# Pack attention and two MoE layers on one core: gate weights in a pool of their own, w_in conversions one per step

## The chip, the cores and the metric

The kernel runs on one core of a Trainium2 chip. The metric is the device time of one execution in microseconds (us); the median of three runs stands for a kernel. An execution was profiled besides; all rows shown come from it. The engines are TensorE (PE; its weight loads are PEld), VectorE (DVE), ScalarE (ACT), GpSimd (POOL) and SyncE (SP), which issues the DMAs.

## The reference

```python
p_packed = sm_attn(p, k, v)              # first attention: 32 packed queries a head, 576 keys
out = sm_attn(q, p_packed, p_packed)     # second attention: 576 queries, 32 packed keys
x = out.transpose(0, 2, 1, 3).reshape(4608, 512)
h = np.maximum(x @ w_in, 0.0)            # MoE 1: 512 -> 2048, squared relu
x = (h * h) @ w_out                      # 2048 -> 512
logits = x @ w_gate + modality_bias[modality_id]     # 8 experts
e_idx = np.argmax(logits, axis=1)
for e in range(8):                       # MoE 2, each token to one expert
    h = np.maximum(x[mask] @ w1[e], 0.0)
    out[mask] = gate_w[mask, None] * (h @ w2[e])
```

Batch 8, 8 heads of 64, 576 positions; 4608 tokens of 512. `w_in` and `w_out` come as float64, `w1` and `w2` as float32.

## The kernel before

**First attention.** The loop at L892 has 16 + 3 steps. `att1(i)` handles a "quad" (four heads of a batch) in four parts, one a step: scores `s` (L296), softmax (L307 to L314), transposes `ta` and `tb` (L319, L320), the product with the values `pq` (L328, L329) with its split into `pphl`. Step i does the scores of quad i and the `pq` of quad i - 3. SyncE loads keys three quads ahead (576 KB each) and values four ahead (576 KB). Keys lie in parts of `wgb` (the buffer of the gate weights, which are needed only later) and in `rows`; values lie in `early`, the memory that later becomes `ring`.

**Conversions.** The float64 weights are read as pairs of 32-bit integers, a 512 KB load for each [128, 512] tile, and `convert` (L197 to L215) rebuilds a float32 value (Square on ScalarE; L202, L205, L208 and L211 on VectorE) and splits it into `hi` (ScalarE, L214) and `lo` (GpSimd, L215). `conv_in` does 16 tiles of `w_in` into `wbt`, two in each of the first eight steps; at step 8 what is left of it is emitted and the tile `head` is allocated. `head` takes the memory of `stage`, which the conversions use as scratch. `conv_out` does the same for `w_out`, over the same slots of `wbt`, with buffers in `wgb` and `rows`; it follows behind the attention.

**Pack products.** `pw_unit(bp, u)` multiplies the packed attention of a pair of batches `bp` with tile `u` of `w_in`: three products (L360), a copy into `pws` (three buffers; on VectorE for odd pairs, L364, else on ScalarE, L366) and a write to DRAM. For pair 0 the halves go straight into the blocks `head` and `ring` (L375 on ScalarE, L376 on GpSimd), which layer 1 reads. The table `PW` says which units are placed in which step; `others(u)` makes what is missing ahead of and in the first token unit, with one `conv_out` step each. In the first attention all of `ta`, `tb`, `pq`, the scores of the second attention and `pw` share four PSUM banks.

**MoE 1** runs over 12 units of 384 tokens and 16 slices `f`: `layer1` (L472), relu and square, `layer2` (L492). `tail(u)` multiplies the rows of a unit with the eight gate weight rows in `wgb`; 24 products with a sum each (L515 on VectorE), then softmax and a write to DRAM; `route` and `tables` assign tokens to expert groups. For the last unit (u = 11), three of eight products a row block go to GpSimd (L519) with the sum on ScalarE (L520).

**MoE 2** runs over nine groups of 512 slots, each with one expert: `gathered` (tokens by indirect DMA, transposed into `xt`), `weights1` and `weights2` (load and split, L720 and L721), and `group`: eight `f` of 12 products (L784), whose relu is split into `ht` by ScalarE (L794) and VectorE (L795), then four times 24 products (L806), scaled into `o` (L815) and scattered (L817). Groups 0 to 6 take tokens of the first 28 of 36 tiles only, so that their tables are made before the last unit's routing.

**Order and memory.** The instructions of each engine are put in order when the kernel is built, by priority and a simulated time line; the order of the code is the priority, and `tc.high_priority` raises it (by 200 instructions for the whole of group 0, by 40 for `ht`). Each engine runs its own list strictly in that order. SBUF pools opened with side "left" stand on one another: ahead of the change `const`, `x2`, `raw`, then, until `st3.close()`, `pp` (`wgb` of 16 KB a partition and `pp32` of 8 KB), `at` and `g`; after that, in their place, `o` (16 KB) and `h` (32 KB). A pool that takes the place of closed ones waits until all instructions that use those are through.

Of the kernel before, what the change touches and what calls it, by code (L numbers as in the profile page):

```python
# [10 lines left out]
F32 = mybir.dt.float32  # L11
# [15 lines left out]
def tile_pack_attention_moe_moe2(  # L27
# [58 lines left out]
    w_p = ctx.enter_context(tc.tile_pool(name="raw", bufs=2, side="left"))  # L86
    pp_p = st3.enter_context(tc.tile_pool(name="pp", bufs=1, side="left"))
# [5 lines left out]
    wgb = pp_p.tile([P, NE, DM], F32, name="wgb")  # L93
# [126 lines left out]
    PW = {9 + i: [(0, 2 * i), (0, 2 * i + 1)] for i in range(4)}  # L220
    PW |= {13 + i: [(1, 2 * i), (1, 2 * i + 1)] for i in range(6)}
    for i in range(3):
        PW[16 + i].append((2, i))
    A20 = 4
# [126 lines left out]
    def pw_unit(bp, u, so=None):  # L351
# [11 lines left out]
        if bp % 2:  # L363
            nc.vector.tensor_copy(so, ph)  # L364
        else:
            nc.scalar.activation(out=so, in_=ph, func=AF.Copy)  # L366
# [140 lines left out]
    def tail(u):  # L507
        js = slice(u * UT, (u + 1) * UT)
        lg = lg_all[:, js, :]
        prod = held["g"].tile([P, DM], F32, tag="ghl", name="prod") if u == NUN - 1 else None  # L510
        for t in range(UT):
            for e in range(NE):
                one = lg[:, t, e : e + 1]
                if prod is None or e < 5:
                    nc.vector.scalar_tensor_tensor(  # L515
                        out=junk, in0=row[:, t, :DM], scalar=1.0, in1=wgb[:, e], op0=ALU.mult, op1=ALU.mult, accum_out=one
                    )
                else:
                    nc.gpsimd.tensor_tensor(out=prod, in0=row[:, t, :DM], in1=wgb[:, e], op=ALU.mult)  # L519
                    nc.scalar.activation(out=prod, in_=prod, func=AF.Copy, accum_out=one)  # L520
                if e % 2 == 1:
                    yield
# [249 lines left out]
    def group(g, more):  # L772
# [27 lines left out]
        for t in range(NTT):  # L800
# [13 lines left out]
            o = held["o"].tile([P, DM], F32, tag="o", name="o")  # L814
# [16 lines left out]
    def pull(gens, n=1):  # L831
        for _ in range(n):
            while gens:
                try:
                    next(gens[0])
                    break
                except StopIteration:
                    gens.pop(0)
# [53 lines left out]
    for i in range(len(quads) + 3):  # L892
# [10 lines left out]
        pull(cv, 2)  # L903
        if i == 8:
            pull(cv, NU)
            held["head"] = const.tile([P, HEAD, 2, NPC, P], F32R, tag="head", name="head")
# [88 lines left out]
    held["o"] = ctx.enter_context(tc.tile_pool(name="o", bufs=8, side="left"))  # L995
# [70 lines left out]
```

## Time and profile before

| what | us |
|---|---|
| median of three runs | 1307.05 (1306.3 to 1307.85) |
| the profiled execution | 1303.67 |
| its span, first to last instruction | 1301.9 |

| engine | busy us | share of the span |
|---|---|---|
| TensorE products | 1232.0 | 95% |
| TensorE weight loads | 1028.0 | 79% |
| VectorE | 811.6 | 62% |
| ScalarE | 607.1 | 47% |
| GpSimd | 336.8 | 26% |

Times in rows are us from the start of the span. "Busy" is the time in which an engine works on an instruction; the granted clock (PEclk) is the share of TensorE's full 2.4 GHz, so that 0.50 is 1.2 GHz. A timeline row merges like instructions that follow one another; `x12` are twelve of them; `<-` in brackets names what ended the wait ahead of it. In a stretch's row each engine's busy time is followed by its count of instructions.

### The profile page before, as it was taken

What the parts mean: (1) busy time and instruction counts of PE and PEld (TensorE: products, weight loads), DVE (VectorE), ACT (ScalarE), POOL (GpSimd) and SP (SyncE); (2) the same over time, 40 slices, a digit from 0 to 9 for tenths busy, and PEclk for the clock granted to TensorE, in tenths of its full rate; (3) what the DMA queues carried; (4) which work ended last, traced back from release to release, by engine and by line L of the source; (5) the groups of instructions that cost most, each with busy time, mean ns of one, the idle gap of its engine ahead of it and who ended that gap; (6) DMA issues with size and microseconds to landing.
All of it is one profiled execution on the core that took longest, in us unless ns stands there. A gap on an engine that the chain in (4) does not pass through costs nothing.

```text
span 1301.9 us, 18383 instructions
## 1 busy us (share of the span) xinstructions
PE 1232.0 (95%) x6356; PEld 1028.0 (79%) x6356; DVE 811.6 (62%) x2022; ACT 607.1 (47%) x1227; POOL 336.8 (26%) x398
## 2 busy tenths in 40 slices
PE   7899899999999999999999999929999999999995
PEld 4567777888888888888888888818788888888884
DVE  5886865849758694874867597875543444354341
ACT  3675565565555555455654556531433332343230
POOL 4663565322103231022310132040220221122011
PEclk8799999999999999999999999969999999999998
DMA  9876656332011221112121023320532542453210
GB/s 348 296 268 212 186 170 181 119 90 75 25 42 49 68 79 43 42 50 66 49 74 43 25 77 97 122 81 10 195 129 77 185 159 91 141 186 98 107 65 35
DMA packets 74167, 145.06 MB, mean 111 GB/s; under 512 B 6608, under 2 KB 26192, under 8 KB 73936
## 3 DMA queue, kind: packets, MB, share of 16 engines
q1 hardware_dynamic: 68304, 124.62, 29.9%
q0 software_dynamic: 5760, 19.17, 4.5%
q8 instruction: 52, 0.85, 0.3%
q14 instruction: 51, 0.42, 0.1%
HBM read 109.92 MB, written 33.85 MB: 110 GB/s over the span
## 4 chain that ended last, share of the span: by engine, by line
PE 84%; DVE 5%; DMA 4%; ACT 2%; POOL 2%; issue 2%; SPq 0%; POOLq 0%; ACTq 0%; DVEq 0%
PE acc L492 28%; PE ph L472 16%; PE h L784 15%; PE o L806 15%; PE pq L328 2%; PE s L427 2%; PE pw L360 2%; DMA wraw<-in_moe_w 2%; PE tr L764 1%; PE s L296 1%; POOL prod L519 1%; DMA wgb<-in_moe_w_out 1%; PE pq L329 1%; DMA rows<-in_moe_w_out 1%; PE ta L454 1%
## 5 line engine op out<-in xcount | busy, mean ns | idle before, releaser
L492 PE MATMUL acc<-wbt,ghl 128*128 128x512 f32 x1728 | 443.5, 399 | 0.0
L492 PEld LDWEIGHTS acc<-wbt,ghl 128*128 128x128 f32 x1728 | 315.9, 189 | 60.6 <-ACT ghl L483 0.4
L515 DVE SCALAR_TENSOR_TENSOR rows<-rows,wgb 128x512 f32<-128x512 f32 x279 | 218.9, 785 | 3.7
L784 PE MATMUL h<-xt,wbt 128*128 128x512 f32 x864 | 215.1, 399 | 0.7 <-DVE xt L768 0.4
L784 PEld LDWEIGHTS h<-xt,wbt 128*128 128x128 f32 x864 | 163.0, 189 | 40.3 <-DVE xt L768 0.7
L485 DVE TENSOR_TENSOR ghl<-r,ghl 128x384 fp32r<-128x384 f32 x176 | 108.0, 615 | 114.0 <-ACT ghl L483 113.2
L472 PE MATMUL ph<-a2T,ring 128*128 128x384 f32 (+1 forms) x840 | 145.7, 310 | 2.3 <-ACT ring L403 2.3
L483 ACT ACTIVATE ghl<-r 128x384 fp32r<-128x384 f32 x192 | 100.2, 522 | 97.5 <-PE acc L492 95.7
L472 PEld LDWEIGHTS ph<-a2T,ring 128*128 128x128 f32 x840 | 130.4, 191 | 10.6 <-ACT ring L403 2.8
L806 PE MATMUL o<-head,ht 128*128 128x512 f32 x432 | 113.9, 398 | 26.0 <-ACT ht L794 25.8
L481 ACT ACTIVATE r<-ph 128x384 f32<-128x384 f32 x192 | 92.9, 485 | 91.1 <-PE ph L472 85.1
L795 DVE SCALAR_TENSOR_TENSOR ht<-h,ht 128x512 fp32r<-128x512 f32 x72 | 49.3, 688 | 124.2 <-ACT ht L794 124.1
L472 PE MATMUL ph<-a2T,head 128*128 128x384 f32 (+1 forms) x696 | 119.4, 308 | 0.0
L806 PEld LDWEIGHTS o<-head,ht 128*128 128x128 f32 x432 | 81.2, 190 | 45.2 <-issue 26.2
L817 POOL DMA_INDIRECT out<-o,idx_s x36 | 36.7, 1018 | 299.3 <-DVE o L815 293.7
L806 PE MATMUL o<-ring,ht 128*128 128x512 f32 x432 | 112.2, 395 | 0.0
L794 ACT ACTIVATE ht<-h 128x512 fp32r<-128x512 f32 x72 | 42.5, 593 | 148.8 <-PE h L784 148.8
L472 PEld LDWEIGHTS ph<-a2T,head 128*128 128x128 f32 x696 | 106.5, 190 | 6.3
L482 ACT ACTIVATE r<-r 128x384 f32<-128x384 f32 x192 | 99.9, 522 | 4.1
L404 POOL TENSOR_TENSOR ring<-praw,ring 128x256 fp32r<-128x256 f32 x62 | 52.2, 843 | 168.8 <-ACT ring L403 123.6
L806 PEld LDWEIGHTS o<-ring,ht 128*128 128x128 f32 x432 | 80.3, 188 | 16.8
L721 DVE TENSOR_TENSOR wbt<-wraw,wbt 128x1024 fp32r<-128x1024 f32 x36 | 44.1, 1225 | 50.0 <-ACT wbt L720 49.8
(213 smaller groups left out, 1482.7 us busy)
## 6 DMA issues: line engine op xcount, KB each, us to landing
wraw<-in_moe_w SPq DMA_DIRECT2D x72, 512.0 KB, 3.7
praw<-pw_d SPq DMA_DIRECT2D x56, 256.0 KB, 3.9
pw_d<-pws SPq DMA_DIRECT2D x48, 256.0 KB, 3.1
x_d<-rows SPq DMA_DIRECT2D x12, 792.0 KB, 4.0
qT<-in_q SPq DMA_DIRECT2D x36, 256.0 KB, 3.7
early<-in_v SPq DMA_DIRECT2D x16, 512.0 KB, 6.6
rows<-in_k SPq DMA_DIRECT2D x10, 576.0 KB, 6.3
wgb<-in_moe_w_out SPq DMA_DIRECT2D x11, 512.0 KB, 4.5
```

What stands on the lines that cost most here:

```text
L404: nc.gpsimd.tensor_tensor(out=t[:, 1], in0=raw, in1=t[:, 0].bitcast(F32), op=ALU.subtract)
L472: nc.tensor.matmul(ph[:, off : off + n], t[:, x, c, :], a[:, y, c, off : off + n], start=(i == 0), stop=(i == 3 * NPC - 1),)
L481: nc.scalar.activation(out=r, in_=ph, func=AF.Relu)
L482: nc.scalar.activation(out=r, in_=r, func=AF.Square)
L483: nc.scalar.activation(out=hl[:, 0], in_=r, func=AF.Copy)
L485: eng.tensor_tensor(out=hl[:, 1], in0=r, in1=hl[:, 0].bitcast(F32), op=ALU.subtract)
L492: nc.tensor.matmul(acc[t], hl[:, x, t * P : (t + 1) * P], wbt[:, f, y, :], start=(f == 0 and x == 0 and y == 0), stop=(f == NF - 1 and x = ...
L515: nc.vector.scalar_tensor_tensor(out=junk, in0=row[:, t, :DM], scalar=1.0, in1=wgb[:, e], op0=ALU.mult, op1=ALU.mult, accum_out=one)
L721: nc.vector.tensor_tensor(out=t[:, 1, :], in0=raw, in1=t[:, 0, :].bitcast(F32), op=ALU.subtract)
L784: nc.tensor.matmul(ph, half1[:, g % 2, c, x, f * P : (f + 1) * P], xs[c][:, y, :], start=(i == 0), stop=(i == 3 * NDC - 1),)
L795: nc.vector.scalar_tensor_tensor(out=h[:, 1, :], in0=ph, scalar=0.0, in1=h[:, 0, :].bitcast(F32), op0=ALU.max, op1=ALU.subtract)
L806: nc.tensor.matmul(po, hs[f][:, x, t * P : (t + 1) * P], second(f)[:, y, :], start=(i == 0), stop=(i == 3 * NFE - 1),)
```

## The change

The gate weights `wgb` get a pool of their own, `wg`, ahead of `pp`, which stays open to the end; `o` in MoE 2 uses the eight 2 KB slices of `wgb` in turn and its own pool goes. The last unit's 24 gate products are all on VectorE. One `w_in` conversion is emitted a step instead of two, to the end of step 15; what follows in `head` comes at step 16. In `PW`, pair 1's units 0 to 11 stand in steps 11 to 16; pair 0's units 0 to 3 and pair 2's units 0 and 1 in steps 17 and 18 (before: pair 0's units 0 to 7 in steps 9 to 12, pair 1's units 0 to 11 in 13 to 18, pair 2's 0 to 2 in 16 to 18). The copies into `pws` are all on ScalarE during the first attention. The second attention of unit 0 starts at step 6 instead of 4.

```diff
--- before.py
+++ after.py
@@ -84,13 +84,14 @@
     st2 = ExitStack()
     st3 = ExitStack()
     w_p = ctx.enter_context(tc.tile_pool(name="raw", bufs=2, side="left"))
+    wg_p = ctx.enter_context(tc.tile_pool(name="wg", bufs=1, side="left"))
     pp_p = st3.enter_context(tc.tile_pool(name="pp", bufs=1, side="left"))
     pw_p = st1.enter_context(tc.tile_pool(name="pw", bufs=1, side="right"))
     a_p = st2.enter_context(tc.tile_pool(name="a1", bufs=2, side="right"))
     
     ident = const.tile([P, P], F32, name="ident")
     make_identity(nc, ident)
-    wgb = pp_p.tile([P, NE, DM], F32, name="wgb")
+    wgb = wg_p.tile([P, NE, DM], F32, name="wgb")
     pp32 = pp_p.tile([P, B, HP, 2 * NPK], F32, name="pp32")
     nc.gpsimd.memset(pp32, 0.0)
     pphl = pw_p.tile([P, PAIRS, 2, HP, 2 * P // 2], F32R, name="pphl")
@@ -217,11 +218,9 @@
     w_in32 = w_in64.bitcast(I32).rearrange("r (f t) -> r f t", t=2)
     w_out32 = w_out64.bitcast(I32).rearrange("r (f t) -> r f t", t=2)
     NU = 4 * HP
-    PW = {9 + i: [(0, 2 * i), (0, 2 * i + 1)] for i in range(4)}
-    PW |= {13 + i: [(1, 2 * i), (1, 2 * i + 1)] for i in range(6)}
-    for i in range(3):
-        PW[16 + i].append((2, i))
-    A20 = 4
+    PW = {11 + i: [(1, 2 * i), (1, 2 * i + 1)] for i in range(6)}
+    PW |= {17 + i: [(0, 2 * i), (0, 2 * i + 1), (2, i)] for i in range(2)}
+    A20 = 6
     PRI = 0
     a2T = {}
 
@@ -360,7 +359,7 @@
             nc.tensor.matmul(ph, hl[:, x, hp], w[:, y, :], start=(i == 0), stop=(i == 2))
         if so is None:
             so = pw_p.tile([P, 512], F32, tag="w5", name="pws", bufs=3)
-        if bp % 2:
+        if bp % 2 and "early" not in held:
             nc.vector.tensor_copy(so, ph)
         else:
             nc.scalar.activation(out=so, in_=ph, func=AF.Copy)
@@ -507,17 +506,12 @@
     def tail(u):
         js = slice(u * UT, (u + 1) * UT)
         lg = lg_all[:, js, :]
-        prod = held["g"].tile([P, DM], F32, tag="ghl", name="prod") if u == NUN - 1 else None
         for t in range(UT):
             for e in range(NE):
                 one = lg[:, t, e : e + 1]
-                if prod is None or e < 5:
-                    nc.vector.scalar_tensor_tensor(
-                        out=junk, in0=row[:, t, :DM], scalar=1.0, in1=wgb[:, e], op0=ALU.mult, op1=ALU.mult, accum_out=one
-                    )
-                else:
-                    nc.gpsimd.tensor_tensor(out=prod, in0=row[:, t, :DM], in1=wgb[:, e], op=ALU.mult)
-                    nc.scalar.activation(out=prod, in_=prod, func=AF.Copy, accum_out=one)
+                nc.vector.scalar_tensor_tensor(
+                    out=junk, in0=row[:, t, :DM], scalar=1.0, in1=wgb[:, e], op0=ALU.mult, op1=ALU.mult, accum_out=one
+                )
                 if e % 2 == 1:
                     yield
         mx = mx_all[:, js]
@@ -811,7 +805,7 @@
                         stop=(i == 3 * NFE - 1),
                     )
                     i += 1
-            o = held["o"].tile([P, DM], F32, tag="o", name="o")
+            o = wgb[:, (g * NTT + t) % NE]
             nc.vector.tensor_scalar(out=o, in0=po, scalar1=gates[t], scalar2=None, op0=ALU.mult)
             s = g * NTT + t
             put = nc.gpsimd.indirect_dma_start(
@@ -900,8 +894,8 @@
         if i == A20:
             bg = [att2(0)]
         pull(bg)
-        pull(cv, 2)
-        if i == 8:
+        pull(cv)
+        if i == NU:
             pull(cv, NU)
             held["head"] = const.tile([P, HEAD, 2, NPC, P], F32R, tag="head", name="head")
         for bp, u in PW.get(i, ()):
@@ -992,7 +986,6 @@
     other = [tail(NUN - 1), route(NTL - UT, NTL)]
     pull(other, 100)
     st3.close()
-    held["o"] = ctx.enter_context(tc.tile_pool(name="o", bufs=8, side="left"))
     held["h"] = ctx.enter_context(tc.tile_pool(name="h", bufs=NFE, side="left"))
     tables(G_A, G_MAX)
```

## Rows read from the trace of the kernel before

**Rows 1.** The page, part 2: TensorE's busy tenths in 40 equal slices.
```profile
PE   7899899999999999999999999929999999999995
```

**Rows 2.** Stretches: us; PE, PEld, DVE, ACT, POOL busy (instructions); PEclk; DMA share; GB/s.
```profile
...
850.00:860.00 10.00, 0.00 (x0) 0.00 (x0) 9.48 (x15) 4.50 (x10) 5.81 (x4) 0.64 0.49 157
860.00:870.00 10.00, 0.00 (x0) 0.00 (x0) 9.69 (x19) 2.89 (x8) 6.67 (x5) 0.50 0.00 0
...
```

**Rows 3.** Timeline, 843 to 883 us: start, duration, engine, line, operation, [idle before].
```profile
843.22 2.96 PE L784 MATMUL h<-xt,wbt 128*128 128x512 f32 x12
...
846.22 2.34 PE L492 MATMUL acc<-wbt,ghl 128*128 128x512 f32 x9
...
857.17 1.57 POOL L519 TENSOR_TENSOR prod<-rows,wgb 128x512 f32<-128x512 f32 x1 [0.83 <-ACT prod L520]
...
857.67 1.62 DVE L515 SCALAR_TENSOR_TENSOR rows<-rows,wgb 128x512 f32<-128x512 f32 x1
...
859.33 0.69 DVE L515 SCALAR_TENSOR_TENSOR rows<-rows,wgb 128x512 f32<-128x512 f32 x1
...
859.95 0.08 DVE L515 DVE_READ_ACCUMULATOR rows<-rows,wgb 128x1 f32 x1
...
873.63 1.09 ACT L794 ACTIVATE ht<-h 128x512 fp32r<-128x512 f32 x2
...
874.33 2.90 PE L806 MATMUL o<-head,ht 128*128 128x512 f32 x6 [25.77 <-ACT ht L794]
...
877.02 4.39 PE L784 MATMUL h<-xt,wbt 128*128 128x512 f32 x12
...
882.17 2.97 PE L784 MATMUL h<-xt,wbt 128*128 128x512 f32 x12
```

**Rows 4.** Busy time by stretch in the first attention; columns as in Rows 2.
```profile
...
40.00:60.00 20.00, 17.47 (x92) 12.15 (x92) 15.36 (x39) 11.36 (x25) 12.39 (x13) 0.73 0.81 264
60.00:80.00 20.00, 19.42 (x127) 14.67 (x125) 18.28 (x49) 15.41 (x33) 11.69 (x12) 1.00 1.00 348
...
```

**Rows 5.** The first attention as one stretch; columns as in Rows 2.
```profile
0.00:131.00 131.00, 109.58 (x623) 79.78 (x623) 93.47 (x220) 72.52 (x146) 66.53 (x95) 0.87 0.81 279
...
```

**Rows 6.** The same, VectorE on L202, L205, L208, L211, L364; then PEclk, DMA.
```profile
0.00:131.00 131.00, 8.67 (x19) 0.87 0.81 279
...
0.00:131.00 131.00, 16.80 (x19) 0.87 0.81 279
...
0.00:131.00 131.00, 16.01 (x19) 0.87 0.81 279
...
0.00:131.00 131.00, 15.75 (x19) 0.87 0.81 279
...
0.00:131.00 131.00, 7.38 (x11) 0.87 0.81 279
```

**Rows 7.** Timeline of TensorE in the first attention; columns as in Rows 3.
```profile
23.95 2.19 PE L296 MATMUL s<-wgb,ptb 128*64 128x288 f32 x8
...
105.43 1.19 PE L296 MATMUL s<-wgb,ptb 128*64 128x288 f32 x8
...
110.06 1.67 PE L360 MATMUL pw<-wbt,pphl 128*128 128x512 f32 x6
...
114.78 1.79 PE L360 MATMUL pw<-wbt,pphl 128*128 128x512 f32 x6
...
130.93 0.43 PE L329 MATMUL pq<-atbuf,early 64*128 64x64 f32 x2
```

**Rows 8.** Timeline of ScalarE around step 8; columns as in Rows 3.
```profile
78.30 0.58 ACT L366 ACTIVATE pws<-pw 128x512 f32<-128x512 f32 x1
...
91.93 1.92 ACT L375 ACTIVATE head<-pws 64x512 fp32r<-64x512 f32 x3
```

**Rows 9.** SyncE's w_out loads (L233): first and last of ten.
```profile
141.15 0.33 SPq L233 DMA_DIRECT2D wgb<-in_moe_w_out  x1
...
192.80 0.40 SPq L233 DMA_DIRECT2D wgb<-in_moe_w_out  x1
```

## Prediction

> **What bounds the kernel now.** Start with the page's forty slices: TensorE is busy nine tenths or more nearly everywhere, so time can be won only where it is not [rows 1]. Two places stand out: slice 27 with a 2, and the first slices. The table of stretches goes into the first of them: from 850 to 870 us TensorE runs nothing at all, VectorE is busy 9.48 and 9.69 of each 10 us, ScalarE only 4.50 and 2.89 [rows 2]. The timeline says what ended the hole: the last product of the first MoE (L492) ends at 848.56, a product of the second (L806) starts at 874.33 after 25.77 us idle, put down to ScalarE's `ht` (L794) [rows 3]. The `h` that L794 reads was finished at 846.18 [rows 3], and ScalarE had free time, so L794 was waiting neither for its input nor for a busy engine. What ends just ahead of it is the last token unit's `tail`: 24 products with the gate weights, 15 on VectorE (L515) and 9 on GpSimd and ScalarE (L519, L520). I read it as a wait for memory: the pool `h` is opened after `st3.close()` and lies where the pool `pp` lay, and `pp` holds `wgb`, which those products read until their end. Nothing in group 0 needs their results; TensorE waits for the place.
>
> In the first attention TensorE is busy 109.58 of 131 us at a mean granted clock of 0.87 [rows 5]. Full-rate work is thus about 109.6 x 0.87 = 95 us, and 36 us are lost to waits and to the 1.2 GHz level (0.73 of full speed on average from 40 to 60 us, 1.00 from 60 to 80 [rows 4]).
>
> **The gap between the stages.** With `wgb` in a pool of its own, `h` lies on `pp32`, `at` and `g` only, and their last reader is the L492 that ends at 848.56. L794 can then run at about 848.7. It takes 0.55 (1.09 for two [rows 3]), VectorE's second half L795 about 0.7, bounded by the 0.69 of a product of the same width [rows 3], and one VectorE instruction may be ahead of it: TensorE resumes near 851, a hole of 2.5 us (1.5 to 6). Saved: 25.8 - 2.5 = 23.3. The hole also cost clock: the twelve L784 after it take 4.39 against 2.97 later, and the six L806 take 2.90 where about half would do [rows 3]; that is 1.4 + 1.4 = 2.8, saved if the hole is too short to bring the clock down, as I take it. Sum 26; I take 25, leaving 1 for VectorE's competition below; ends 21 and 27.
>
> The nine products that move to VectorE cost 0.69 + 0.08 = 0.77 each when GpSimd is still; beside a running `prod` (1.57) the same instruction takes 1.62 [rows 3]. So VectorE needs 24 x 0.77 = 18.5 us instead of 15 products at a mix of both. They are costed at nothing: only late groups need the routing that follows. Their cover is the rest of group 0, some 39 us of TensorE work from 874.33 in which VectorE has `ht`, `xt` and `o` alone. Queued behind a product on VectorE is at most one L795, so each costs at most 0.77, under one L784 dozen (2.97 [rows 3]). If that cover fails, it is the second rival. The `o` tiles inside `wgb` are eight buffers as before and cost nothing; the first waits for the last read of its slice, under the same cover.
>
> Perfetto Trace Analysis in the Trainium skill (section Optimizing Scalar/DVE Operations) says that with a saturated VectorE it may make sense to offload to ScalarE or even GpSimd, and adds that GpSimd shares a read port with VectorE, so it might not help. Its first half speaks against this change; the 1.62 beside 0.69 in rows 3 sides with the second half. By the first half alone I would count nine moved products as a loss, 9 x 0.77 = 7 us if they were on the path; by the rows I count none.
>
> **The first attention.** The w_in conversions go from two in each of the first eight steps to one in each of sixteen. One costs VectorE (8.67 + 16.80 + 16.01 + 15.75) / 19 = 3.0 us [rows 6] (19, since three w_out conversions lie in the stretch). All else on VectorE is 93.5 - 57.2 - 7.4 = 28.9 [rows 5, 6], or 1.8 a step. A step therefore needs 4.8 us of VectorE throughout, where before it needed 7.8 and then 1.8. At the highest share that VectorE reaches, 18.28 of 20 [rows 4], that is 5.3. Data: 1152 KB of keys and values and a 512 KB conversion tile are 1.70 MB, at 348 GB/s [rows 4] 4.9 us. TensorE: two pack units, one `pq` and one transpose take 114.78 - 110.06 = 4.7, scores 1.19, a pack unit 1.67 / 2 = 0.83 [rows 7]; so 4.3 without pack units and 5.9 with two. Three engines near their limits don't overlap perfectly: I take 5.6 for steps 3 to 10 and 6.1 for 11 to 14.
>
> The start does not change: step 3's scores stay at 23.95 [rows 7]. Step 11 comes at 24 + 8 x 5.6 = 69, step 15 at 69 + 4 x 6.1 = 93 (before: 105.43). From there to the end of the last `pq` it took 131.4 - 105.4 = 25.9 before [rows 7], with some three pack units more: I take 23, so the stage ends at 116, 15 us sooner. Five pack units of TensorE work (four of pair 0, one of pair 2) have left for the next stage: 5 x 0.83 = 4. Net 11.
>
> Part of this is a jam that goes. Pair 0's `pws` is ready at 78.30, but its `head` block is written only at 91.93, when the last w_in conversion has given up the memory [rows 8]; three `pws` buffers and then PSUM banks stand full meanwhile. Behind the conversions, pair 0 waits no more. What is late next: layer 1 needs `head` blocks written in the very last steps. TensorE has pack units left to cover that, eight or more at 0.83.
>
> What is queued behind: on SyncE, keys and values stand in one queue with the conversion loads, which now come one a step; on GpSimd, four `lo` halves of pair 0 move past the stage's end and lie beside TensorE work. The moved copies (L364, 7.4 us off VectorE [rows 6]) find ScalarE idle 58 of 131 us [rows 5]: nothing, 7 us if that cover were gone. `att2(0)` two steps later: nothing, since layer 1 needs it only after step 18.
>
> A loss: w_out conversions can't start before the last w_in one. Before, they loaded from 141.15 to 192.80 in nine gaps of 5.7 us [rows 9], on or near the path. One of them that used to be ahead and now is not costs between 0 and 5.7; I take 1, since VectorE is freer in steps 16 to 18. **Net of the stage: 10 us won.** Ends: 20 won (steps at the data's 4.9), 6 lost (no step faster, one conversion on the path).
>
> **The sum.** 25 + 10 = 35. The profiled execution took 1303.67, its span 1301.9; 1303.67 - 35 = 1268.7. The median of the runs, 1307.05, stands 3.4 above it: **1272**.
>
> **Rivals.**
> First, the front gives nothing: faster steps are handed back to the w_out conversions, which start with VectorE's queue full and pace layers 1 and 2 at 5.7 each [rows 9]. For it: that pace is close to TensorE's own. Against it: VectorE was busy only 93.5 of 131 us [rows 5]. Time 1307 - 25 = 1282.
> Second, the place is not free after all, or L795 is ordered behind all 24 products on VectorE. Then `ht` waits for 18.5 us of products and one or two weight splits: TensorE resumes near 870.5, 4 us sooner than 874.33. Against it: only one `wgb` reader is left near `h`, and group 0 is emitted with higher priority. Time 1307 - 4 - 10 = 1293.
> Third, slower: the granted clock. Between steps 3 and 15 TensorE now gets its work in thinner portions. If it stays at 1.2 GHz, scores take 2.19 instead of 1.19 [rows 7], a factor 1.84: the steps become 8 x 4.3 x 1.84 + 4 x 5.9 x 1.84 = 107 and step 15 comes at 131, and if the rest follows at half rate, 23 becomes 42 and the stage ends at 173, 42 later plus 4 for the moved units. Time 1307 + 46 - 25 = 1328. It decides from the point where the low clock outlasts step 14: until there the gap's 25 pays for it. For it: 0.73 between 40 and 60 us; against it: 1.00 from 60 to 80 in the same mix of small products [rows 4].
>
> **How the numbers follow.** Forecast 0.65 (its own range 1260 to 1285), first rival 0.18, second 0.08, third 0.05, others 0.04. The likeliest gives 1272. The low end is 1307 - 27 - 20 = 1260; the high end takes in the first rival with its worst front and a gap of 21: 1307 - 21 + 6 = 1292. Outside lie the third, half of the second and others, under 2 in 10. A measurement of this kernel can tell about 0.2% from no change: faster 0.92 (forecast, first, second, a little more), same 0.03, slower 0.05.
>
> **What would show it.** In the changed profile: L806 or L784 right behind the last L492 with under 6 us idle and a granted clock of 1.00 there; L515 at 0.69 throughout and spread over group 0; no L519 or L520; step 15's scores near 93 and the last `pq` near 116; L375 on `head` without a wait of ten us after its `pws`. I am wrong if L794 still stands behind the last L515, if step 15 is at 105 or later, or if a new hole opens in front of the first L492.

## The result, and the profile after

| kernel | median us | lowest to highest | profiled execution | its span | its granted clock |
|---|---|---|---|---|---|
| before | 1306.67 | 1305.84 to 1307.85 | 1303.67 | 1301.9 | 0.972 |
| after | 1295.32 | 1293.57 to 1296.13 | 1296.13 | 1294.3 | 0.964 |

These medians are of four runs each. The ratio is 0.9911 [0.9893, 0.9928]: 11 us faster. The forecast was 1272; the time lies 3.3 us above the upper end of its range, 1292. The sign and the gap between the MoE stages were right; the first attention was not. What stood at 35 us won came out as some 24 won in the gap and 9 to 13 lost in front.

Line numbers after are lower by one to six: L492 is now L491, L784 L778, L806 L800, L794 L788, L515 L512.

In the forty slices of after the 2 of [rows 1] is gone. The granted clock has its low digits, 7, 6, 7 and 8, in the first four slices, the first attention:

```profile
PE   7899898999999999999999999989999999999995
...
PEclk7678999899999999999999999999999999999998
```

The stretches of after (columns as in rows 2); the second and third answer to [rows 4], the last two lie around the gap:

```profile
0.00:134.00 134.00, 117.41 (x603) 88.13 (x603) 84.96 (x209) 69.81 (x143) 50.44 (x88) 0.76 0.79 267
40.00:60.00 20.00, 19.53 (x89) 14.86 (x89) 17.30 (x35) 10.47 (x22) 10.12 (x13) 0.56 0.69 217
60.00:80.00 20.00, 19.48 (x101) 14.00 (x100) 16.04 (x40) 11.32 (x24) 6.87 (x9) 0.66 0.89 303
860.00:870.00 10.00, 6.68 (x31) 4.95 (x31) 7.78 (x19) 5.12 (x7) 0.00 (x0) 1.00 0.47 159
870.00:880.00 10.00, 10.00 (x38) 7.89 (x38) 8.61 (x23) 0.71 (x2) 0.00 (x0) 0.83 0.15 54
```

Read the first row beside [rows 5]. TensorE is busy for more of the stage (117.4 of 134 us against 109.6 of 131) and yet does less: 117.41 x 0.76 = 89 us of full-rate work by 134 us, where before had 109.58 x 0.87 = 95 by 131. A busy engine at a low clock looks full on the page; only the two columns together show the loss.

The timeline of TensorE, ScalarE and VectorE at the gap in after:

```profile
861.67 3.65 PE L491 MATMUL acc<-wbt,ghl 128*128 128x512 f32 x15
865.17 0.41 PE L656 MATMUL pl<-od,om 128*128 128x184 f16 x3
...
866.82 1.06 ACT L714 ACTIVATE wbt<-wraw 128x1024 fp32r<-128x1024 f32 x1 [1.67 <-DMA wraw<-in_moe_w]
...
868.26 1.08 ACT L788 ACTIVATE ht<-h 128x512 fp32r<-128x512 f32 x2
...
868.90 2.13 PE L800 MATMUL o<-head,ht 128*128 128x512 f32 x6 [3.31 <-ACT ht L788]
870.83 4.13 PE L778 MATMUL h<-xt,wbt 128*128 128x512 f32 x12
...
871.02 0.68 DVE L512 SCALAR_TENSOR_TENSOR rows<-rows,wgb 128x512 f32<-128x512 f32 x1
```

The 25.77 us of [rows 3] are 3.31. The gate products (L512) begin only when ScalarE's `ht` is under way and stand between group 0's own work at 0.68 to 0.69 each. TensorE's order is aligned product by product between the two traces: after is 16.8 us late at the last product of the first MoE and 7.6 us early at the last of the second. The gap is therefore worth 24.4 us, and the 17 us were lost before it, all of them by the start of unit 1 (252 us): 6.8 by the first layer-1 product, 8.8 within unit 0, the rest at its end. The profiled execution of before is 3.0 us shorter than its median, so the aligned traces show more of the loss than the medians do.

Of the prediction's signs for the front, the scores of step 15 start at 112.03 (forecast 93, before 105.43) and the last `pq` ends at 134.2 (forecast 116, before 131.4). "Step 15 at 105 or later" was one of its signs of being wrong.

### The profile page after: what moved, and what is told of

Read it like the earlier page. It is cut to its first block, busy times and chain, and to the rows that moved or that the text cites. A ratio compares the mean times of both kernels' runs of the same rounds, so it can differ in the third digit from the quotient of the medians.

```text
span 1294.3 us, 18381 instructions
## 1 busy us (share of the span) xinstructions
PE 1247.8 (96%) x6356; PEld 1042.2 (81%) x6356; DVE 808.2 (62%) x2028; ACT 606.2 (47%) x1221; POOL 314.2 (24%) x389
## 4 chain that ended last, share of the span: by engine, by line
PE 87%; DVE 4%; DMA 4%; ACT 2%; issue 2%; POOL 1%; SPq 0%; POOLq 0%; ACTq 0%; DVEq 0%
PE acc L491 28%; PE ph L471 15%; PE h L778 15%; PE o L800 15%; PE pq L327 3%; PE s L426 2%; PE pw L359 2%; PE s L295 1%; DMA wraw<-in_moe_w 1%; DMA wgb<-in_moe_w_out 1%; PE tr L758 1%; PE pq L328 1%; PE ta L318 1%; DVE wgb L206 1%; PE ta L453 1%
## 5 line engine op out<-in xcount | busy, mean ns | idle before, releaser
L491 PE MATMUL acc<-wbt,ghl 128*128 128x512 f32 x1728 | 443.9, 399 | 2.1 <-ACT ghl L482 1.7
L491 PEld LDWEIGHTS acc<-wbt,ghl 128*128 128x128 f32 x1728 | 317.1, 189 | 63.3 <-ACT ghl L482 1.8
L512 DVE SCALAR_TENSOR_TENSOR rows<-rows,wgb 128x512 f32<-128x512 f32 x288 | 217.3, 754 | 3.9
L778 PE MATMUL h<-xt,wbt 128*128 128x512 f32 x864 | 214.6, 398 | 0.0
L778 PEld LDWEIGHTS h<-xt,wbt 128*128 128x128 f32 x864 | 162.7, 189 | 39.1 <-DVE ht L789 0.2
L789 DVE SCALAR_TENSOR_TENSOR ht<-h,ht 128x512 fp32r<-128x512 f32 x72 | 49.2, 688 | 117.4 <-ACT ht L788 117.3
L811 POOL DMA_INDIRECT out<-wgb,idx_s x36 | 36.4, 1012 | 341.7 <-DVE wgb L809 251.6
L800 PE MATMUL o<-head,ht 128*128 128x512 f32 x432 | 112.7, 396 | 3.5 <-ACT ht L788 3.3
L788 ACT ACTIVATE ht<-h 128x512 fp32r<-128x512 f32 x72 | 42.3, 592 | 148.6 <-PE h L778 148.6
L800 PE MATMUL o<-ring,ht 128*128 128x512 f32 x432 | 111.6, 394 | 0.0
L800 PEld LDWEIGHTS o<-head,ht 128*128 128x128 f32 x432 | 80.3, 188 | 22.4 <-ACT ht L788 3.7
L800 PEld LDWEIGHTS o<-ring,ht 128*128 128x128 f32 x432 | 80.4, 188 | 16.9
```

Source lines behind the costliest of these rows:

```text
L491: nc.tensor.matmul(acc[t], hl[:, x, t * P : (t + 1) * P], wbt[:, f, y, :], start=(f == 0 and x == 0 and y == 0), stop=(f == NF - 1 and x = ...
L512: nc.vector.scalar_tensor_tensor(out=junk, in0=row[:, t, :DM], scalar=1.0, in1=wgb[:, e], op0=ALU.mult, op1=ALU.mult, accum_out=one)
L778: nc.tensor.matmul(ph, half1[:, g % 2, c, x, f * P : (f + 1) * P], xs[c][:, y, :], start=(i == 0), stop=(i == 3 * NDC - 1),)
L789: nc.vector.scalar_tensor_tensor(out=h[:, 1, :], in0=ph, scalar=0.0, in1=h[:, 0, :].bitcast(F32), op0=ALU.max, op1=ALU.subtract)
L800: nc.tensor.matmul(po, hs[f][:, x, t * P : (t + 1) * P], second(f)[:, y, :], start=(i == 0), stop=(i == 3 * NFE - 1),)
```

## Experiments: the two parts apart

**The gap alone.** The kernel before with the new pool and the tail on VectorE, the first attention untouched:

```diff
+    wg_p = ctx.enter_context(tc.tile_pool(name="wg", bufs=1, side="left"))
...
-    wgb = pp_p.tile([P, NE, DM], F32, name="wgb")
+    wgb = wg_p.tile([P, NE, DM], F32, name="wgb")
...
-            o = held["o"].tile([P, DM], F32, tag="o", name="o")
+            o = wgb[:, (g * NTT + t) % NE]
...
-    held["o"] = ctx.enter_context(tc.tile_pool(name="o", bufs=8, side="left"))
```

and the hunk of `tail` as in the change.

> The kernel before with the gate weights in a pool of their own, o in their slices, and the last unit's 24 products on VectorE; the first attention is that of before. Theory (the two parts of the change add up: the gap is worth 24.5 us by the aligned traces, the front costs 17): the hole between the stages is about 3 us, the front is that of before (scores of step 15 at 105, first layer-2 product at 141), and the time is 1307 - 24 = 1283 (1280 to 1286), below both kernels. Rival (the gain of the gap hangs on VectorE being free there only because the front moved work, or is given back later in MoE 2): about 1295, as the changed kernel.

Measured 1282.9, ratio 0.9819 [0.9796, 0.9842]; on another chip, beside the runs further down, 1286.16, 0.9836 [0.9804, 0.9868]:

> The kernel with the gap closed and the first attention of before, on the same chip as the three that follow, as their common base: 1281 to 1286, ratio to the kernel before 0.982.

The hole is 3.41 us here, with the first attention of before:

```profile
853.21 2.33 PE L802 MATMUL o<-head,ht 128*128 128x512 f32 x6 [3.41 <-ACT ht L790]
```

This half of the change is faster than the whole by 9 to 12 us. No other kernel of the study is clearly faster than it. Its two medians, one from each chip, differ by 3.3 us; that is the scale on which the smaller differences below have to be read.

**The front alone.** The other hunks (`PW`, `A20`, the copies, `pull(cv)`) on the kernel before.

> The kernel before with the front part of the change alone (one conversion a step, the moved pack products, all pws copies on ScalarE, the second attention from step 6); the gate weights stay in pp and the last unit's products stay split. Theory (the front costs what the aligned traces show): 1307 + 17 = 1324 (1320 to 1328), the hole of 25.8 us between the MoE stages as before. Rival (the loss in front only exists together with the new pool, for instance through memory moved in the first attention): about 1307.

Measured 1317.57, 1.0063 [1.0041, 1.0084]: 10 us slower, less than the 1320 to 1328 expected, which had been taken from the profiled executions. The two parts add up within a few us: 24.7 won, 9.9 lost, 14.8 against the 11.4 of the whole.

**The tail alone.** Only the hunk of `tail`; `wgb` stays in `pp`.

> The kernel before with the last unit's 24 products all on VectorE, and no pool for the gate weights. Theory (the wait is one for the memory under the pool h, held by the last reader of the gate weights in pp): h still waits for the last product, which now ends after 24 x 0.77 = 18.5 us instead of some 23; TensorE resumes near 870 and the time is 1302 to 1304. Rival (it was only GpSimd's and ScalarE's share of the products that stood ahead of ht, and the pool does nothing): TensorE resumes near 852 and the time is 1283.

Measured 1305.78, 0.999 [0.9978, 1.0003], above the theory's 1302 to 1304. The hole is nearly whole. Its timeline (TensorE, ScalarE, VectorE's last product):

```profile
852.94 0.41 PE L657 MATMUL pl<-od,om 128*128 128x184 f16 x3
875.42 2.93 PE L801 MATMUL o<-head,ht 128*128 128x512 f32 x6 [22.07 <-ACT ht L789]
...
874.77 1.08 ACT L789 ACTIVATE ht<-h 128x512 fp32r<-128x512 f32 x2 [18.11 <-DVE rows L513]
...
873.96 0.69 DVE L513 SCALAR_TENSOR_TENSOR rows<-rows,wgb 128x512 f32<-128x512 f32 x1
```

With all 24 products on one engine, ScalarE still sits idle for 18.11 us until the last of them has ended, and then runs `ht` at once. Nothing of ScalarE's or GpSimd's own order held it; what the pool takes away is the wait for the last reader of `wgb`. The 24 products take from 857.03 to 874.65, 17.6 us. In before the split form starts 6 us sooner and ends at much the same place; its first product on GpSimd and its last sum on ScalarE:

```profile
850.98 1.81 POOL L519 TENSOR_TENSOR prod<-rows,wgb 128x512 f32<-128x512 f32 x1 [47.68 <-ACT rows L505]
...
873.41 0.19 ACT L520 ACTIVATION_READ_ACCUMULATOR prod<-prod 128x1 f32 x1
```

That is 22.6 us for the split form, with one weight split of 1.22 on VectorE among it. So the offload that the Trainium skill (Perfetto Trace Analysis, section Optimizing Scalar/DVE Operations) allows for a saturated VectorE made the stretch longer here, and the time no shorter; that page's doubt about GpSimd is what the trace bears out.

The pool without the change of `tail` was not tried, and it may not have been enough: `prod` lies in the pool `g`, which is closed together with `pp`, and in before `ht` starts at 873.63, right behind the last L520 in ScalarE's own order.

## Experiments: the conversions

**Two a step again.** The changed kernel with the old pace:

```diff
-        pull(cv)
-        if i == NU:
+        pull(cv, 2)
+        if i == 8:
```

> The changed kernel with two w_in conversions a step as before (and the head's memory taken at step 8); the new order of the pack products, the copies on ScalarE, the start of the second attention and the new pool stay. Theory (the pace of one conversion a step makes the front slow: TensorE busy 20 of 20 us at a granted clock near 0.6 from 40 to 80 us): the scores of step 15 come near 105 again, the clock is 1.00 at 60 to 80 us, and most of the 17 us come back: about 1283 (1280 to 1287). Rival (the loss is in the five pack units that moved into the next stage and the order of the pairs): it stays at 1292 to 1297.

Measured 1297.8, 0.9922 [0.99, 0.9944]: the rival's side, if 0.8 above its range. To see the pace without the other pieces, the gap-only kernel got the new `PW` alone, and then also one conversion a step:

> The kernel before with its gap closed (1283 us) and one piece of the front: pair 1's pack units first (steps 11 to 16), pair 0's first four and two of pair 2 in steps 17 and 18, five units less in the first attention; two conversions a step, second attention from step 4, copies as before. Theory P: the five units and the late head blocks cost what the aligned traces show behind the stage's end, 17 - 3 = 14 us less what the later start of the second attention hides: 1291 to 1297. Theory A: five units of 0.83 us, 1287.

> As the run that moves only the pack units, and one w_in conversion a step instead of two: the changed kernel without its later start of the second attention and without its ScalarE copies. If the forecast's reason for the front was right (thinner conversions free VectorE), it is some 10 us below the run with the pack units alone. If conversions are not what bounds the steps (the changed kernel with two a step was within 2 us of the one with one), the two are within 3 us of each other.

Measured 1289.62, between the two theories, and 1289.53. The two are the same kernel but for the pace, and the pace did not reach the chip: TensorE, GpSimd and SyncE run their instructions in the same order in both. The conversions on VectorE's first line (L203; durations in ns, then first and last start in us), two a step:

```profile
L203 DVE TENSOR_SCALAR stage<-stage x5: 409/508/617, 27.6 to 85.7; 128x512 int32<-128x512 int32 x5
L203 DVE TENSOR_SCALAR wgb<-stage x3: 409/414/509, 30.0 to 92.2; 128x512 int32<-128x512 int32 x3
```

and one a step:

```profile
L203 DVE TENSOR_SCALAR stage<-stage x5: 409/508/612, 27.8 to 85.8; 128x512 int32<-128x512 int32 x5
L203 DVE TENSOR_SCALAR wgb<-stage x3: 414/415/506, 30.2 to 92.4; 128x512 int32<-128x512 int32 x3
```

The sixteenth starts at 92.2 or 92.4. In the kernel before it starts at 88.6, in step 13, and not at the end of step 8:

```profile
L202 DVE TENSOR_SCALAR wgb<-stage x3: 414/427/507, 26.9 to 88.6; 128x512 int32<-128x512 int32 x3
```

The line in the source says in which step a conversion is emitted, and not when it runs. What does set that (its load, the four raw buffers, the order laid out for each engine) was not tested apart.

## Experiments: which piece of the front costs

Each row is one kernel. "First" is the start of the first layer-1 product in the profiled execution, "unit 0" the time from there to the start of the last group of layer-2 products of the first unit, "layer 1" the time from there to the end of that unit's last layer-1 product, "clock" the mean granted clock of the profiled execution.

| kernel | median us | ratio to before | first | unit 0 | layer 1 | clock |
|---|---|---|---|---|---|---|
| gap only (two groups of runs) | 1282.9, 1286.16 | 0.9819, 0.9836 | 135.6, 138.9 | 88.9, 90.6 | 98.0, 100.2 | 0.981, 0.976 |
| + second attention from step 6 | 1291.62 | 0.9873 [0.9839, 0.9908] | 143.9 | 89.4 | 99.6 | 0.968 |
| + copies on ScalarE | 1291.82 | 0.987 [0.9843, 0.9898] | 143.0 | 96.4 | 103.7 | 0.972 |
| + new `PW` | 1289.62 | 0.9863 [0.9838, 0.9889] | 133.0 | 98.1 | 107.8 | 0.976 |
| + new `PW`, one conversion a step | 1289.53 | 0.986 [0.9838, 0.9881] | 135.6 | 96.9 | 107.0 | 0.975 |
| changed kernel | 1295.32 | 0.9911 [0.9893, 0.9928] | 141.3 | 97.8 | 108.1 | 0.964 |
| changed, second attention from step 4 | 1288.07 | 0.9853 [0.9824, 0.9882] | 130.9 | 98.7 | 108.5 | 0.980 |
| changed, copies on VectorE | 1293.54 | 0.9886 [0.9854, 0.9919] | 135.7 | 98.4 | 108.3 | 0.971 |
| changed, `PW` of before | 1295.3 | 0.9902 [0.9876, 0.9928] | 142.6 | 95.1 | 102.0 | 0.969 |

**One piece added** (edits: `A20 = 6`; `and "early" not in held` on the copies; the third, `PW`, stands above):

> The kernel before with its gap closed (own pool for the gate weights, tail on VectorE, 1283 us) and one piece of the front: the second attention of unit 0 starts at step 6 instead of 4. Theory A (that late start takes work from TensorE while it waits for data at 24 to 60 us, so the granted clock of that stretch stays near 0.6 and all later steps come late): scores of step 3 at 29 instead of 25, scores of step 15 at 112, about 1290 (1287 to 1295). Theory P (what costs is the five pack units that moved into the next stage): 1283 to 1286.

> The kernel before with its gap closed (1283 us) and one piece of the front: all pws copies of the first attention on ScalarE. Theories A and P: nothing, 1281 to 1285, since ScalarE is idle for more than a third of the stage. Rival: ScalarE's in-order queue holds the attention's own copies, +7.4 us (the busy time that leaves VectorE), 1290.

Against the two groups of runs of the gap-only kernel, the second attention alone costs 5 to 9 us, the copies 6 to 9 and `PW` 3 to 7. The gap-only kernel was not run on the chip of these three. The copies were costed at nothing, and neither theory had expected their loss; the rival named beside them had (7.4), but its reason, ScalarE's queue, was not tested. The three sum to 15 to 24, more than the 9 to 12 of the whole, so they overlap; that was looked at by taking one away.

**One piece taken from the changed kernel:**

> The changed kernel with the second attention of unit 0 from step 4 again, the rest of the front as changed. If the later start is what the first 140 us of the changed kernel lose (its granted clock stays at 0.50 until 56 us and falls back at 68), 1287 to 1291 and the first layer-1 product near 135 us instead of 141; unit 0 still takes 97. If not, 1293 to 1297.

> The changed kernel with pair 1's copies on VectorE again, the rest as changed. If the ScalarE copies cost by themselves (8.9 us when they were the only piece of the front), 1285 to 1289. If they cost nothing beside the other pieces, 1293 to 1297.

> The changed kernel with the pack products in the places of before (and so two conversions a step and the head's memory at step 8); the later second attention and the ScalarE copies stay. If the order and number of the pack units is what unit 0 of the first MoE loses (97.8 us against 88.9), unit 0 takes 89 to 90 us and the time is 1286 to 1291. If not, 1293 to 1297.

Only the start of the second attention gives back a clear amount, 7 us. The intervals of the other two overlap that of the changed kernel. The column "unit 0" has 95 to 99 us with the new copies, with the new `PW` or with both, and 89 to 91 with neither. But it ends at the start of a group of nine products that runs through in 2.3 us in both kernels with the copies on ScalarE and the `PW` of before, and is spread over 6 to 8 us in the others. The column "layer 1" has no such break: 107 to 109 us with the new `PW` whatever the copies, 102 to 104 with the copies alone, 98 to 100 with neither. So taking back the copies leaves the whole of `PW`'s loss in unit 0. Taking back `PW` saves 6 us there, of which the median shows nothing; 1.3 go in the later start of layer 1, and where the rest goes is not shown. In part, what unit 0 loses through `PW` the front wins back, because four pack units (63 pack products instead of 75) lie behind the first layer-1 product instead of ahead of it.

TensorE's waits in unit 0 of the changed kernel (us in total, times, longest):

```profile
PE pw L359 <- DVE pws L363: 5.6, 4, 2.3
PE acc L491 <- ACT ghl L482: 1.7, 1, 1.7
```

and of the gap-only kernel:

```profile
PE pw L361 <- DVE pws L365: 2.2, 2, 1.2
PE s L428 <- ACT pws L367: 1.5, 2, 1.3
```

Four units at 0.83 are 3.3 us of work; the waits on VectorE's `pws` are 3.4 more. Together that is 6.7 of the 8.9 by which unit 0 is longer.

**The pack units by number and by order.** Gap-only kernel with, first, pair 1 ahead, all units kept (pair 0's eight in steps 16 to 18; these lines follow the first line of the new `PW`) and one conversion a step; second, the order of before and the last five units dropped; third, the order of before and three units more:

```diff
+    PW[16] += [(0, i) for i in range(2)]
+    PW[17] = [(0, i) for i in range(2, 5)] + [(2, 0)]
+    PW[18] = [(0, i) for i in range(5, 8)] + [(2, 1), (2, 2)]
```

```diff
-    PW |= {13 + i: [(1, 2 * i), (1, 2 * i + 1)] for i in range(6)}
-    for i in range(3):
-        PW[16 + i].append((2, i))
+    PW |= {13 + i: [(1, 2 * i), (1, 2 * i + 1)] for i in range(5)}
```

```diff
-    for i in range(3):
-        PW[16 + i].append((2, i))
+    for i in range(6):
+        PW[16 + i // 2].append((2, i))
```

> The kernel with the gap closed (1283 us); pair 1's pack units first as in the changed kernel, one conversion a step, but no unit leaves the first attention: all eight of pair 0 and three of pair 2 stand in steps 16 to 18. Theory U (what costs is the number of pack units left for unit 0 of the MoE: 21 done ahead of the first layer-1 product against 25, and unit 0 then takes 97 us instead of 89): unit 0 takes 89 us again and the time is 1282 to 1286. Rival O (the order costs: pair 0's head blocks come late, so layer 1 and the ring wait): unit 0 stays near 97 us and the time is 1288 to 1292.

> The kernel with the gap closed (1283 us), the order of before (pair 0 first), and the last five pack units taken out of the first attention (two of pair 1, three of pair 2), so that unit 0 has to do them. Theory U: the first layer-1 product some 4 us sooner, unit 0 at 96 to 98 us, 1287 to 1291. Rival O: unit 0 near 90 to 93 us, the time 1282 to 1285.

> The kernel with the gap closed (1283 us), the order of before, and three more pack units of pair 2 (six instead of three) in steps 16 to 18. Theory U, carried on: 28 units ahead of the first layer-1 product, which starts 2.5 us later, and unit 0 shorter by 5 to 7: 1277 to 1281, the fastest of all. Rival (25 units are already enough, unit 0 is bound by its w_out conversions at 5.7 to 6 us each): unit 0 stays near 89 and the time is 1284 to 1287.

Measured 1288.84 (0.984 [0.9803, 0.9876]), 1290.64 (0.9846 [0.9809, 0.9883]) and 1287.72 (0.9829 [0.9792, 0.9865]). Unit 0 took 92.7, 95.9 and 89.5 us with 78, 63 and 87 pack products ahead of it, and 99.4, 104.2 and 96.5 to the end of its layer 1, where the gap-only kernel has 98.0 and 100.2 with 75. By the second measure fewer units ahead lengthen unit 0 whatever the order, as theory U has it. The times do not follow: the first came out in rival O's range, and the third, for which U had 1277 to 1281, gained nothing. The work that unit 0 is spared stands ahead of it instead. The intervals of the three overlap one another and that of the gap-only kernel, so order against number is not settled in the total time.

## Experiments: why a later start costs 7 us

The start of the second attention changes the order of TensorE's work near step 3. Gap-only kernel, from step 4, timeline of TensorE:

```profile
22.58 1.97 PE L329 MATMUL pq<-atbuf,early 128*128 128x64 f32 x8
24.48 0.69 PE L330 MATMUL pq<-atbuf,early 64*128 64x64 f32 x2
25.09 2.19 PE L297 MATMUL s<-wgb,ptb 128*64 128x288 f32 x8
27.07 1.56 PE L297 MATMUL s<-rows,ptb 128*64 128x288 f32 x8
28.56 1.10 PE L428 MATMUL s<-pp,qT 128*128 128x64 f32 x8
```

From step 5:

```profile
22.52 1.97 PE L329 MATMUL pq<-atbuf,early 128*128 128x64 f32 x8
24.42 0.69 PE L330 MATMUL pq<-atbuf,early 64*128 64x64 f32 x2
25.04 1.97 PE L329 MATMUL pq<-atbuf,early 128*128 128x64 f32 x8
...
27.55 1.97 PE L329 MATMUL pq<-atbuf,early 128*128 128x64 f32 x8
29.45 0.69 PE L330 MATMUL pq<-atbuf,early 64*128 64x64 f32 x2
30.07 2.19 PE L297 MATMUL s<-wgb,ptb 128*64 128x288 f32 x8
```

Twenty-four `pq` products of L329 instead of eight run ahead of the scores of step 3, as in the changed kernel (there the scores start at 29.10).

> The kernel with the gap closed and the second attention of unit 0 from step 3 instead of 4. If an earlier start brings the scores of step 3 ahead of the narrow pq products and so keeps the low clock short, 1280 to 1286, scores of step 3 by 23 us, and the clock at 1.00 from 52 us or sooner. If step 4 is only one lucky order among several, 1288 to 1293.

> The kernel with the gap closed and the second attention of unit 0 from step 5. If the loss goes with the order (24 pq products ahead of the scores of step 3, as with step 6), it is like step 6: the clock at 0.50 until 56 to 68 us and 1289 to 1293. If it grows with the delay, 1285 to 1289.

Step 3: 1286.86 (0.9833 [0.9802, 0.9865]), as with step 4; the scores of step 3 start at 22.67, but the clock's rise came only after 56 us, later than expected, and from 68 to 80 us it is back at 0.57. Step 5: 1297.89 (0.9899 [0.9862, 0.9936]), no better than step 6 (0.9873). Run side by side, the six runs of step 3 lie between 1286.56 and 1288.94, those of step 5 between 1291.77 and 1300.79. It is a jump with the order, not a slope with the delay. The stretch from 44 to 68 us (columns as in rows 2), from step 4:

```profile
44.00:68.00 24.00, 23.42 (x129) 15.99 (x128) 18.89 (x55) 14.16 (x32) 13.87 (x14) 0.84 0.86 296
```

and from step 5:

```profile
44.00:68.00 24.00, 24.00 (x100) 17.85 (x100) 17.81 (x42) 11.48 (x24) 10.06 (x11) 0.50 0.68 226
```

TensorE is busy without a break for 24 us in the second and gets 1.2 GHz throughout; 100 instructions end where the first had 129, and the DMAs move less (226 GB/s against 296). At 23.42 x 0.84 = 19.7 against 12.0 that is 7.7 us of full-rate work. It is not the whole account, for the two executions are 18 us apart (1280.33 and 1298.53). Nor does this stretch part the two orders cleanly: its clock is 0.69 in another execution from step 4, 0.71 from step 3, and 0.64 in the changed kernel. The whole first attention parts them better; from step 3 and from step 5:

```profile
0.00:131.00 131.00, 110.21 (x597) 81.59 (x598) 94.42 (x219) 70.75 (x145) 62.60 (x95) 0.82 0.81 273
0.00:131.00 131.00, 111.28 (x525) 80.96 (x526) 86.83 (x200) 68.12 (x135) 62.54 (x92) 0.70 0.76 259
```

TensorE is busy about as long in both, and does 110.21 x 0.82 = 90 us of full-rate work in one and 111.28 x 0.70 = 78 in the other. The 12 us between them are about what these two executions differ by (1286.56 and 1298.53). So between these two the loss is a low clock and not waiting. That the order of step 3 is what keeps the clock low fits the medians of all these kernels; it is not shown, since from step 3 too the clock was low until 56 us and from 68 to 80.

To see whether other work can lift the clock, twelve products of 512 columns that nothing reads were added in steps 5 to 7 of the kernel from step 6:

```diff
+        if i in (5, 6, 7):
+            dead = bank("t", "dead")
+            for k in range(4):
+                nc.tensor.matmul(dead, wbt[:, 0, 0, :P], wbt[:, 0, 0, :], start=(k == 0), stop=(k == 3))
```

> The kernel with the gap closed and the second attention from step 6 (1291.6 us), with twelve more TensorE products of 512 columns (on a converted weight, into a bank that nothing reads) in steps 5 to 7. They are added work of 12 x 0.55 = 6.6 us at the low clock. If it is the make-up of TensorE's work (only narrow products of 64 to 288 columns between 44 and 68 us) that keeps the granted clock at 0.50 there, the clock reaches 1.00 some 10 us sooner and the time is 1284 to 1290 in spite of the added work. If the make-up has nothing to do with it, the time is 1294 to 1300.

Measured 1289.69 (0.9845 [0.9801, 0.9889]); without them it was 1291.62 (0.9873). Its stretch:

```profile
44.00:68.00 24.00, 22.32 (x147) 17.27 (x148) 22.79 (x53) 14.44 (x31) 11.69 (x12) 0.93 0.82 277
```

The clock is at 0.93 there instead of 0.50, and added work cost no time: that fits the first case. The products also changed the order of what follows them, and the intervals overlap, and it is one execution, so it is support and not proof.

## Why the prediction was wrong, point by point

- **The gap: right.** Forecast 25 (21 to 27), measured 24.4 by the aligned products and 21.5 to 24.7 by the medians. The hole is 3.31 instead of 2.5: one weight split (L714, 1.06 at 866.82) and a copy stood ahead of L788 on ScalarE. The clock did still fall once: the first twelve L778 take 4.13, against 4.39 and 2.97 in [rows 3], so of the 2.8 put on clock 0.3 came from L778 and 0.8 from the six L800 (2.13 against 2.90).
- **The nine products at nothing: right.** L512 at 0.69 throughout, spread over group 0; the tail alone moved nothing. Whether the pool would have closed the gap without them is open (above).
- **The conversions: the step that failed first.** "A step therefore needs 4.8 us of VectorE throughout, where before it needed 7.8 and then 1.8" took the emission for the execution. The trace of before would have shown it: L202 runs there from 18 to 88.6 us, one about every 4.7, over steps 3 to 13; and [rows 8] was read as a jam although its own 91.93 says that the last conversion came then and not in step 8. The forecast's 11 us of faster steps had nothing to come from: step 15 came at 112.03 and not at 93, and one or two a step measured 1289.53 and 1289.62.
- **"`att2(0)` two steps later: nothing": wrong, some 7 us.** Only its results were costed, not the order that it changes. It is the largest term of the loss that was shown by undoing it.
- **The moved copies and pack units: mis-sized.** They were put at 0 and 4, and w_out at 1. Unit 0 takes 97.8 us where it took 89.0 (108.1 and 97.9 to the end of its layer 1), and the w_out loads follow one another at 6.7 us (147.36 to 207.62 in nine gaps) instead of the 5.7 of [rows 9]. That the two together, less the four us that the shorter front gets back, are the rest of the 9 to 12 is argued: taken away singly they gave back 2 and 0.
- **The third rival had the low clock, for another reason, and got too small a chance.** The granted clock did stay low (0.56 from 40 to 60, 0.66 from 60 to 80, against [rows 4]). But TensorE's work did not come in thinner portions: it was busy for more of the stage, and the pace of the conversions changed nothing. Its price was put at 46 us and a chance of 5 in 100; it came at 7 to 11, inside a kernel that is faster by the gap. The row that was held against it, 1.00 from 60 to 80 "in the same mix of small products", was one execution's: the kernel with the copies on ScalarE runs the same order there and had 0.66.
- **The range.** Its worst front was 6 lost, and nearer 7 by its own terms (2.9 won at the stage's end, 4 for the moved units, 5.7 for a conversion); 9 to 12 were lost. An end for "the order of TensorE's work in front changes" was missing.

## What to carry to other kernels

A change of the step in which something is emitted is no change of when it runs: look first at the start times of those very instructions in the trace, and count no gain on a pace that they don't show. Where a change also reorders a stage near TensorE's limit, multiply busy time by granted clock before and after, and keep an end of the range for it. And undo the parts of a mixed change one by one in both directions: three pieces that each cost 3 to 9 us alone gave back 7, 2 and 0 when taken away.

## What the runs showed of the hardware that was not expected

- **A stretch without a break at half the clock.** TensorE, busy in 24.00 of 24 us, ran at 0.50 throughout (above). The Trainium skill (TensorE: Matmul & The Clock Gate, section Part 1: The HAM clock gate) puts it as "the default state is throttled, and activity releases the throttle"; if busy time counts as activity, the trace does not bear that out: the clock was not released in these 24 us.
- **The clock differs between executions of one kernel, and between kernels in the same instructions.** The gap-only kernel had 0.84 from 44 to 68 us in the execution above (1280.33) and 0.69 in another (1287.41):

```profile
44.00:68.00 24.00, 23.42 (x109) 15.68 (x108) 14.81 (x42) 12.58 (x29) 11.12 (x11) 0.69 0.72 243
```

With the copies on ScalarE, the order of every engine's instructions is that of the gap-only kernel until 107 us. Its scores at 63 us nevertheless run at the low clock:

```profile
62.41 0.66 PE L329 MATMUL pq<-atbuf,early 128*128 128x64 f32 x4 [0.58 <-ACT atbuf L322]
63.00 1.23 PE L297 MATMUL s<-wgb,ptb 128*64 128x288 f32 x4
64.16 0.69 PE L329 MATMUL pq<-atbuf,early 128*128 128x64 f32 x2
```

where the gap-only kernel, after the same instructions and the same 0.58 us of waiting, has the full one:

```profile
64.26 0.66 PE L329 MATMUL pq<-atbuf,early 128*128 128x64 f32 x4 [0.58 <-ACT atbuf L322]
64.85 0.71 PE L297 MATMUL s<-wgb,ptb 128*64 128x288 f32 x4
65.49 0.43 PE L329 MATMUL pq<-atbuf,early 128*128 128x64 f32 x2
```

The scores of step 15, which run before anything of that edit does, start at 111.68 with the copies on ScalarE, at 106.55 and 110.02 in the two executions of the gap-only kernel and at 105.43 in before [rows 7], all in one and the same order. So up to 5 us of the 143.0 in the table are not the copies' doing. A few us in this stage are the clock's and not the kernel's, and one profile can't price a piece there; medians over several runs do it only roughly. What sets the moment at which the clock rises stays open.
